# New hand-out order for five engines in an attention and MLP kernel

## The chip, the cores and the metric

The kernel runs on one NeuronCore of a Trainium2 chip. The metric is the device time of one launch in microseconds. Before the change the median of three runs is 753.31 us (754.21, 751.6 and 753.31). A core has five engines that matter here: TensorE (PE, matrix products; the profile shows its weight loads apart, as PEld), VectorE (DVE), ScalarE (ACT), GpSimd (POOL) and SyncE (SP), which in this kernel does nothing but issue transfers. Each engine works through its own instruction stream in the order written and stops where an instruction waits for another engine or for a transfer.

## The reference

A block with conditional layer norm, memory-augmented attention and a squared-ReLU MLP, batch 1, 2048 tokens, width 512, 32 heads of width 16, attention in four segments of 512 tokens, MLP width 1792, all in float32:

```python
mod = (_silu(c) @ w_mod).reshape(...)             # sa, ca, ga, sb, cb, gb
h = _layernorm(x) * (1 + ca) + sa
for s in range(4):                                # segments
    logits = qs @ ks^T * scale + causal mask      # 512 x 512 for each of 32 heads
    a_dot = softmax(logits) @ vs
    a_mem = (phi(qs) @ M) / (phi(qs) @ z + 1e-6)  # memory of the earlier segments
    o = g * a_mem + (1 - g) * a_dot
    M, z = M + phi(ks)^T @ vs, z + sum(phi(ks))
x = x + ga * (o @ wo)
h = _layernorm(x) * (1 + cb) + sb
x = x + gb * (relu(h @ w1 + b1)^2 @ w2 + b2)
```

## The kernel before, in words

**Precision and products.** A float32 factor of the large products is split into a high and a low part, and three products (high·high, high·low, low·high) stand in for one. The projections (`bqk` line 797, `bv` line 867), the output projection (`bwop` line 1287) and the MLP's second product (`bpf` lines 1591 to 1593) do this directly. The MLP's first product (`bh` line 1529) is done by seven products of half-size sums of blocks instead of eight, each of them six matmuls in one PSUM bank.

**Attention.** The work goes by segment and by groups of eight heads, and inside those by quads of four heads. `a_quad` scores a quad once (`ba`, line 905) to find the row maxima: DVE masks and reduces (line 910), the maxima are turned on PE (`bat`, line 970) and brought by SP into the row of the operand tile `ST` that subtracts them (line 978, `ST<-mt`). `b_quad` scores again with the maximum in place (`bpb`, line 1074), ACT takes the exponential (line 1091, `pt`), POOL zeroes what is above the diagonal (line 1078), and PE multiplies with V (`bpv`, line 1133) and turns the result (`bfin`, line 1168). The operands come as follows: `bqk` writes 64 rows at a time in two halves, with an empty ACT node between them (`fence`, line 771) so that the second half starts after the first has finished; ACT and DVE split the result into `sg` (lines 828 and 830), and SP lays it into `ST` with 192 transfers (line 846, `ST<-sg`). `mem` (line 983) reads the memory (`bmr`), turns phi of the keys (`bpkt`, line 1023) and adds to the memory (`bmu`, line 1035).

**MLP.** For each segment and each of seven pairs of 128 columns, `ffn1` gives seven `bh` products; ACT (line 1555) and DVE (lines 1548 and 1552) read each of them out of its bank and add them up, DVE squares (line 1565) and splits (line 1575) the result, and `ffn2` adds it into four output banks, one per 128 tokens, held for the whole segment. The weights of a pair are prepared earlier: POOL and DVE form the sums and SP writes them to memory and fetches them again (line 753, `w1d<-X1L`).

**What sets the order.** The kernel is described as a graph of 3935 nodes, each a few instructions of one engine. `Plan.run` (line 295) walks through it in a time of its own and writes down an order, and `Plan.emit` (line 392) issues the instructions in that order, with nothing else deciding. Which node an engine takes next is not left to priorities: the table `ORDER` (line 57) lists, for each of the five engines, its nodes by number, and the engine takes the next of its list when what the node needs is ready and the buffers it wants are free:

```python
given = self.given.get(e, ())
if turn[e] < len(given):
    n = self.nodes[given[turn[e]]]
    n = n if n in ready[e] and self.can(n) else None
    turn[e] += n is not None
```

Buffers and PSUM banks are handed out first in, first out (`take`, line 280), so another order also gives other buffer numbers to the same work. There are eight banks in all.

Of the kernel before, what the change touches and what calls it, by code (L numbers as in the profile page):

```python
# [69 lines left out]
1498-1499 1208 1240 1500-1501 1236 1144 1248 1503-1504 1243 1331 1505 1220 1506 1325 1481 1338 1482 1346 1483 1560  # L70
1484 1328 1322 1252-1254 1256 1486 1259 1263 1487 1349 1488 1334 1489 1343 1617 1352 1618 1515 1619-1620 1266 1271
1523 1622-1624 1355 1529 1625 1520 1275-1277 1752-1753 1368 1279 1371 1754-1755 1536 1544 2039 2043 1757 1375 1557
1378 1758 1526 1759 1383 1760 1547 2035 2047 1387 1532 1550 1563 1388-1389 1541 1650 1692 1391 1887 1398 1888 1401
1889 1655 1394 1890 1664 1406 1892 1661 1410 1566 1893 1569 1894 1553 1895 1658 1671 1411-1412 1676 1573 1576 1685
1695 1585 1682 1581 1586 1589 1827 1667 1587 1698 1592 1679 1596 1599 1414 1785 1608 1604 1790 1701 1609 1830 1793
1704 1610 1708 2051 1711 1799 2052 1716 2053 1688 2054 1806 1820 1612 1720-1721 1833 1722 1724 1814 2056 1727 2057
1796 1731 2058 1734 1962 1739 2059 1817 1802 1743-1745 1811 2080 1920 1928 2081 1836 2082 1823 2083 1934 1843 1747
2085 1851 2086 1846 2087 1839 2088 1925 2209-2210 1931 2156 1941 2211-2212 1949 1937 1855-1857 1955 1859 2214 1952
2215 2114 2216 1965 2217 2119 1862 2097-2098 1866 2099-2100 1946 1869 2102 1874 2103 1958 2125 2104 2135 2105 2149
2146 496 1878-1880 1971 2128 2333 1974 2334 1978 2140 2335 2122 2336 1981 1882 2338-2339 1986 2143 2340 2131 2341 2259  # L80
2270 1990-1992 1994 2264 2457 2152 2458 1997 2273 2001 2459-2460 2004 2280 2009 2462-2463 2238 2246 2013 2267 2159
2464-2465 2243 2162 2014-2015 2166 2249 498 2169 2017 2174 2178 2182 2185 1968 2179 2252 2276 2180 2189 2192 2404 2197
2599 2615 2201 2362 2255 2202-2203 2373 2602-2604 2367 2605 2205 2607-2608 2283 2609-2610 2290 2631 2293 2618-2619
2376 2620-2621 2286 2370 2623-2624 2298 2625-2626 2634-2635 2383 2397 2636-2637 2379 2647 2302-2304 2486 2494
2639-2640 2306 2641-2642 2500 2663 2313 2650-2652 2321 2653 2666-2667 2316 2668 2491 2669 2655-2656 2391 2657-2658
2309 2671-2673 2497 2674 2407 2727 2679 2325-2327 2730-2733 2410 2388 2414 2735-2738 2682 2394 2683 2422 2684-2685
2743 2687 2400 2688 2507 2689-2690 2521 2746-2749 2417 2329 2751-2752 2430 2753 2433 2754 2426 2515 2503 2437 2695
2800 2796 2804 2792 2427 2449 2428 2759 2440 2698-2699 2445 2700-2701 2518 2531 2703-2705 2512 2706 2534 2711
2450-2451 2762 2538 2524 2763-2765 2453 2546 2767-2768 2541 2769-2770 2714-2716 2554 2557 2717 2775 2550-2551 2561
2564 2719-2721 2528 2569 2722 2552 2573-2575 2778-2781 2577 2783-2786 2934 2933 2935 2839 2936-2937 2859 2842-2845  # L90
2849 2862 2829 2863 2938 2864 2852 2865 2939 2832-2833 2853-2854 2834 2855 2835 2957 2956 2958 2961 2959-2960 2962
3176 3097 2979 3094 2982 3095 2980 3096 2984 3099-3100 2981 3098 3104 3164 2983 2985 3101 3106 3002-3003 3102 3008
3004 3110 3112 3111 3005-3007 3108 3026 3114 3025 3028 3116 3027 3172 3113 3118 3031 3030 3029 3115 3119 3168 3122
3048 3117 3050 3049 3123 3053 3120-3121 3051 3054 3125 3052 3071 3129 3073 3072 3124 3077 3127 3126 3131 3074 3076
3133 3130 3128 3135 3204 3132 3136 3134 3075 3206 3139 3137 3207 3140 3208 3141 3144 3205 3145 3143 3138 3148 3231
3149 3209 3147 3156 3210 3153 3429 3142 3225-3226 3146 3227 3150 3229 3228 3230 3352 3421 3159 3246 3249 3247 3354
3351 3248 3433 3252 3358 3251 3250 3353 3267 3355 3357 3268-3269 3425 3271 3365 3270 3370 3363 3272 3359 3288 3273
3356 3289 3361 3291 3367 3290 3369 3374 3368 3293-3294 3372-3373 3378 3292 3371 3312 3376-3377 3309 3314 3311 3310
3382 3375 3381 3313 3380 3330 3333 3379 3386 3331 3315 3385 3384 3390 3332 3336 3383 3387-3388 3394 3334 3389 3335
3391 3462 3461 3690 3393 3465 3463 3398 3392 3682 3397 3395 3402 3464 3678 3396 3400 3399 3404 3467 3406 3466 3416  # L100
3401 3482 3405 3413 3483-3484 3486 3485 3403 3407 3410 3488 3487 3504 3508 3609-3610 3505 3503 3507 3608 3509 3611
3506 3612 3615 3524 3527 3526 3525 3614 3620 3616 3613 3529 3626 3622 3528 3546 3686 3618 3627 3624 3530 3628 3549
3630 3625 3545 3629 3632 3548 3547 3551 3631 3550 3636 3634 3567 3635 3638 3633 3637 3566 3568-3569 3571 3642 3641
3639 3645 3570 3588 3572 3587 3590 3649 3589 3646 3640 3643 3592 3644 3653 3591 3648 3647 3719 3593 3651 3650 3721
3652 3654 3656 3718 3655 3720 3657 3724 3658-3659 3723 3662 3722 3739 3660 3741 3740 3742 3663 3673 3664 3745 3661
3670 3667 3744 3743 3868 3763 3761 3760 3867 3872 3762 3765-3766 3871 3865 3764 3869 3866 3870 3781 3877 3783 3875
3873 3784 3782 3879 3785-3786 3882 3884 3881 3787 3803 3883 3802 3804 3808 3888 3892 3887 3886 3806 3805 3807 3891
3895 3826 3890 3885 3896 3823 3900 3825 3889 3894 3824 3899 3827-3828 3893 3897 3844 3829 3903 3898 3902 3848 3904
3901 3907 3846 3845 3847 3906 3849-3850 3908 3910 3912 3905 3911 3914 3916 3909 3913 3918 3924 3920 3930 3915 3919
3927 3917 3921  # L110
""",
    "ACT": """
1 4 57 65 96 106 79-80 84 87-88 92 116 108 98 250 118 120 122 100 256 102 258-259 409 110 414 416 310 309 418-419 295
128 112 6 568 301 300 304 303 302 306-307 330-331 326-327 305 131 573 575 578 352 577 278 351 138 357 356 364 363
366-367 436 435 290 360 359 287 286 288 283 289 284 371 285 372 347-348 141 694 838 834 830-831 511 510 835 457 456
380 383 382 379 377 387 386 145 390 699 452-453 701 389 481 395 842 394 704 839 703 595 594 400 636-637 148 843 516
515 522-523 518 849 519 155 526 530-531 763 525 762 473-474 854 615 860 857 489 856 616 863 862 536 539 158 546 545
541-542 538 548 611-612 1018 549 505 721 720 554 553 162 507 559 642 641 648-649 1023 1029 652 651 1032 1031 882
# [1530 lines left out]
```

## Time and profile before

| | before |
|---|---|
| median of three runs | 753.31 us (751.6 to 754.21) |
| span of the profiled execution | 748.9 us |
| instructions in it | 18830 |
| PE busy | 736.3 us (98%) |
| PEld busy | 602.8 us (80%) |
| DVE busy | 585.4 us (78%) |
| ACT busy | 433.4 us (58%) |
| POOL busy | 320.9 us (43%) |

The profile is of one execution, and its own time is its span, 748.9 us. The median of the runs stands 4.4 us above it. Line numbers are those of the kernel before. In the rows of a timeline the first two numbers are the start and the length in microseconds; "x4" is the number of instructions put together in the row, and a bracket at the end is the time that the engine stood idle before it and what it waited for. SPq is SP issuing a transfer. The first 430 us are mostly attention, with weight preparation beside it; from 450 us on it is the MLP.

### The profile page before, as it was taken

The page shows a single profiled execution, that of the slowest core. Times are in us where ns is not written, and L with a number is a line of the kernel's source. Part 1 is how long each engine was busy: PE and PEld are TensorE (multiplying, and loading weights), DVE is VectorE, ACT ScalarE, POOL GpSimd, SP SyncE. Part 2 cuts the span into 40 slices and gives each one's busy share as a digit, 9 for nine tenths or more (in the row PEclk, how much of TensorE's full clock was granted, in tenths as well). Part 3 has the DMA queues.
Part 4 walks back from the last instruction along what each step waited for, and adds up shares of the span by engine and source line. Part 5 has one row for each costly group of instructions (what it writes and reads, how often), then busy time and mean ns, then how long its engine had stood idle before and what let it go on. Part 6 is the DMA issues. An engine that isn't in the chain of part 4 may idle for free.

```text
span 748.9 us, 18830 instructions
## 1 busy us (share of the span) xinstructions
PE 736.3 (98%) x7045; PEld 602.8 (80%) x7045; DVE 585.4 (78%) x1597; ACT 433.4 (58%) x971; POOL 320.9 (43%) x400
## 2 busy tenths in 40 slices
PE   8999999999999999999999999999999999999997
PEld 7876778666877678675888789998998898989986
DVE  5587897989899888799999868878766775576544
ACT  2669888899979987788768835562312311221110
POOL 5667858589968787374324433241020002000000
PEclk9999999999999999999999999999999999999999
DMA  9777763446645354547721366753644354538721
GB/s 310 230 236 238 243 198 90 133 136 191 172 136 136 93 140 139 126 131 221 220 79 59 123 222 248 271 208 107 222 163 181 119 208 182 184 131 280 269 94 56
DMA packets 61060, 129.70 MB, mean 173 GB/s; under 512 B 8613, under 2 KB 23977, under 8 KB 59178
## 3 DMA queue, kind: packets, MB, share of 16 engines
q1 hardware_dynamic: 60818, 128.37, 53.8%
q8 instruction: 56, 0.92, 0.5%
q14 instruction: 34, 0.28, 0.1%
q10 hardware_dynamic: 152, 0.13, 0.1%
HBM read 81.29 MB, written 20.19 MB: 136 GB/s over the span
## 4 chain that ended last, share of the span: by engine, by line
PE 77%; DMA 6%; POOL 4%; ACT 4%; issue 3%; SPq 3%; DVE 2%; POOLq 0%; ACTq 0%
PE bh L1529 19%; PE bpv L1133 7%; PE bpf L1592 7%; PE bpf L1591 7%; PE bpf L1593 7%; PE bqk L797 6%; PE bpb L1074 5%; PE bwop L1287 5%; PE ba L905 4%; PE bv L867 4%; DMA w1d<-X1L 2%; SPq L846 2%; ACT pt L1091 1%; PE bwot L1261 1%; POOL WQK L711 1%
## 5 line engine op out<-in xcount | busy, mean ns | idle before, releaser
L910 DVE CUSTOM_DVE_ANT_0 ba<-ba,msk 128x384 f32<-128x384 f32 (+2 forms) x384 | 192.4, 532 | 25.1 <-PE ba L905 13.7
L1091 ACT ACTIVATE pt<-bpb 128x512 f32<-128x512 f32 x320 | 172.5, 617 | 14.9 <-PE bpb L1074 13.2
L1078 POOL TENSOR_SCALAR_AFFINE_SELECT pt<-pt 128x512 f32<-128x512 f32 x128 | 79.1, 636 | 72.3 <-ACT pt L1091 62.1
L797 PE MATMUL bqk<-HT,WQK 64*128 64x512 f32 x720 | 103.9, 396 | 0.0
L1133 PE MATMUL bpv<-pt,VT 128*32 128x128 f32 (+3 forms) x1024 | 81.1, 437 | 1.1 <-ACT pt L1091 0.4
L1074 PE MATMUL bpb<-ST 64*128 64x256 f32 (+2 forms) x512 | 79.1, 344 | 1.4 <-ACT pt L1091 0.4
L797 PEld LDWEIGHTS bqk<-HT,WQK 64*128 64x128 f32 x720 | 71.4, 185 | 8.8 <-issue 0.9
L905 PE MATMUL ba<-ST 63*128 63x256 f32 (+2 forms) x512 | 76.4, 340 | 2.0 <-DMA ST<-sg 1.3
L1074 PEld LDWEIGHTS bpb<-ST 64*128 64x128 f32 x512 | 51.5, 185 | 20.8 <-ACT pt L1091 4.3
L1573 ACT CAST ST<-xx 128x512 fp32r<-128x512 f32 x43 | 26.5, 620 | 69.3 <-DVE xx L1565 55.0
L905 PEld LDWEIGHTS ba<-ST 63*128 63x128 f32 x512 | 51.0, 185 | 18.5 <-issue 4.9
L1529 PEld LDWEIGHTS bh<-ST 128*128 128x128 f32 x420 | 56.5, 189 | 3.6
L1529 PE MATMUL bh<-ST 128*128 128x256 f32 x420 | 59.2, 282 | 0.0
L1529 PEld LDWEIGHTS bh<-ST,w 128*128 128x128 f32 x420 | 55.7, 190 | 3.1
L1529 PE MATMUL bh<-ST,w 128*128 128x256 f32 x420 | 57.7, 282 | 0.0
L867 PE MATMUL bv<-WVO,HT 64*128 64x512 f32 x384 | 56.9, 397 | 0.0
L1360 POOL TENSOR_TENSOR tt<-h2raw 128x512 f32<-128x512 f32 x8 | 11.0, 1388 | 102.8 <-ACT h2raw L1325 77.6
L1133 PEld LDWEIGHTS bpv<-pt,VT 128*32 128x32 f32 x1024 | 28.1, 109 | 33.4 <-issue 22.8
L910 DVE DVE_READ_ACCUMULATOR2_ANT mx<- 128x1 f32 x384 | 54.2, 141 | 0.0
L1591 PE MATMUL bpf<-w,ST 128*128 128x512 f32 x132 | 52.2, 396 | 0.0
L1592 PE MATMUL bpf<-w,ST 128*128 128x512 f32 x132 | 52.0, 394 | 0.0
L1593 PE MATMUL bpf<-w,ST 128*128 128x512 f32 x132 | 51.7, 391 | 0.0
(204 smaller groups left out, 1600.7 us busy)
## 6 DMA issues: line engine op xcount, KB each, us to landing
ST<-w1d SPq DMA_DIRECT2D x14, 1792.0 KB
w<-w1d SPq DMA_DIRECT2D x14, 1792.0 KB
ST<-sg SPq DMA_DIRECT2D x192, 128.0 KB
w1d<-X1L SPq DMA_DIRECT2D x21, 512.0 KB
xt<-in_A_x SPq DMA_DIRECT2D x16, 256.0 KB
wm<-in_w_mod SPq DMA_DIRECT2D x16, 256.0 KB
xw<-in_A_x SPq DMA_DIRECT2D x16, 256.0 KB
X1L<-in_B_w SPq DMA_DIRECT2D x7, 512.0 KB
```

Of the source, the lines that this page charges most:

```text
L797: nc.tensor.matmul(bank(banks[w]), W3(w, k, x, cols.start, cols.stop)[r], HT[r, y, k], start=first and i == 0, stop=last and i == 2)
L867: nc.tensor.matmul(bank(banks[t]), HT[r, x, k, (t2 + t) * P:(t2 + t + 1) * P], WVO[r, k, y], start=first and i == 0, stop=last and i == 2)
L905: nc.tensor.matmul(dst[:, c0:c0 + n], ST[b:b + 63, 0, sl, qt * P:(qt + 1) * P], ST[b:b + 63, 1, sl, :n], start=True, stop=True)
L910: nc.vector.tensor_tensor_reduce(i, i, msk[:, 512 - n:], scale=1.0, scalar=-3e38, op0=ALU.add, op1=ALU.max, accum_out=o)
L1074: nc.tensor.matmul(dst, ST[b:b + 64, 1, sl, kb * P:(kb + 1) * P], ST[b:b + 64, 0, sl, q0:512], start=True, stop=True)
L1078: nc.gpsimd.affine_select(out=ap, in_=ap, pattern=[[0, ap.shape[1]], [1, P]], compare_op=ALU.is_ge, fill=0.0, base=0, channel_multiplier=-1)
L1091: ns = [op("ACT", 0.49, lambda j=j: nc.scalar.activation(buf("PPP"[n], pt)[:, i + j], bank(keys[j]), AF.Exp, scale=0.25), pr[slot] + 0.01 ...
L1133: nc.tensor.matmul(bank(o)[32 * hq:32 * hq + 32, q0:q0 + src.shape[1]], v[:, a:a + 32], src, start=start, stop=stop, tile_position=(0, 32 ...
L1529: nc.tensor.matmul(pb(i), A[:, x, kk], B[:, y, kk], start=kk == j == 0, stop=kk == 1 and j == 2)
L1591: nc.tensor.matmul(q, rh, wh, start=(i == 0), stop=False)
L1592: nc.tensor.matmul(q, rh, wl, start=False, stop=False)
L1593: nc.tensor.matmul(q, rl, wh, start=False, stop=(i == NF - 1))
```

## The change

Only the table `ORDER` is replaced. The five new lists hold the same nodes, each on the same engine; the graph, the instructions of each node, the buffers and every constant stay. The lists are the result of another search over the same plan, one in which the durations of the nodes were drawn anew again and again instead of being fixed.

The diff is 337 lines long, nearly all of it numbers; its head:

```diff
 ORDER = {
     "PE": """
-8-30 3 31-33 56 34-37 58 64 82 78 38 66 39-40 90 86 41-47 246-249 252-255 405-408 291 410-413 292-293 308 322 294
...
+8-24 3 25-33 56 34-37 58 64 38-39 82 78 66 90 40-43 86 44-47 252 246-249 253-255 405-408 410-413 291-293 308 294 322
...
```

Compared as lists, PE has 1325 nodes, of which 696 stand at another position, most of them by one to three places and at most by 25; of its 1324 pairs of neighbours 568 are kept. On ACT 642 of 955 nodes have moved, on DVE 643 of 907 (by up to 66 places), on POOL 261 of 342, on SP 346 of 403 (by up to 46). Between the products that use full precision in different ways PE changes over 140 times in the old list and 142 times in the new one. In the built programs PE has 327 separate wait instructions before and 313 after. Three places follow.

**First place: SP, about 290 to 305 us.** These are transfers into the operand tile (`ST<-sg`, line 846), the maxima's rows (`ST<-mt`, line 978), a write of prepared weights (`w1d<-X1L`, line 753), the modulation weights (`wm`, line 564) and the attention output on its way through memory (`o_dram<-on`, line 1195). Before:

```order
L978 DMA ST<-mt 1x8x128 x2
L564 DMA wm<-in_w_mod 128x512
L846 DMA ST<-sg 32x2x512 x3
L564 DMA wm<-in_w_mod 128x512 x2
L846 DMA ST<-sg 32x2x512 x2
L564 DMA wm<-in_w_mod 128x512
L753 DMA w1d_136<-X1L 256x1x512
L846 DMA ST<-sg 32x2x512 x3
L1195 DMA o_dram<-on 128x4x128
L846 DMA ST<-sg 32x2x512 x3
L978 DMA ST<-mt 1x8x128 x2
```

And now:

```order
L978 DMA ST<-mt 1x8x128 x2
L564 DMA wm<-in_w_mod 128x512
L846 DMA ST<-sg 32x2x512 x4
L1195 DMA o_dram<-on 128x4x128
L846 DMA ST<-sg 32x2x512 x3
L978 DMA ST<-mt 1x8x128 x2
L846 DMA ST<-sg 32x2x512 x3
L753 DMA w1d_136<-X1L 256x1x512
```

Between the two pairs of `ST<-mt` the weight write is gone (it stands behind them), three of the four `wm` loads are elsewhere, and seven fills are listed instead of eleven. The fill of line 846 that stands first in the last row of three of the old list, the 15th transfer after the first pair, is in the new list the third of the row of three, the ninth transfer after it; the PE node that uses it, a `ba` pair, stands two nodes earlier in PE's list.

**Second place: PE, about 45 to 56 us.** `ba`, `bpb` and `bpkt` are the attention products named above, `bv` the projection of V. Before:

```order
L867 MATMUL bv<-WVO,HT 128x512 x12
L905 MATMUL ba_686<-ST 128x512
L905 MATMUL ba_687<-ST 128x512
L867 MATMUL bv<-WVO,HT 128x512 x6
L1023 MATMUL bpkt<-ident,phi_377 128x64 x8
L867 MATMUL bv<-WVO,HT 128x512 x6
L905 MATMUL ba_736<-ST 128x256
L905 MATMUL ba_737<-ST 128x256
L905 MATMUL ba_736<-ST 128x384
L905 MATMUL ba_737<-ST 128x384
L1074 MATMUL bpb<-ST 128x512 x2
```

And now:

```order
L867 MATMUL bv<-WVO,HT 128x512 x12
L905 MATMUL ba_690<-ST 128x512
L905 MATMUL ba_691<-ST 128x512
L867 MATMUL bv<-WVO,HT 128x512 x12
L1023 MATMUL bpkt<-ident,phi_448 128x64 x8
L1074 MATMUL bpb<-ST 128x512 x2
L867 MATMUL bv<-WVO,HT 128x512 x6
L1074 MATMUL bpb<-ST 128x256 x2
L1074 MATMUL bpb<-ST 128x384 x2
L1074 MATMUL bpb<-ST 128x256 x2
L1074 MATMUL bpb<-ST 128x384 x2
L867 MATMUL bv<-WVO,HT 128x512 x6
```

Two groups of `bv` stand ahead of `bpkt` instead of one, and the four `ba` that followed it stand behind the end of the `bpb` shown.

**Third place: PE in the MLP's last segment.** `bh` is the first product, six matmuls to a bank, and `bpf` the second. The longest row of `bh` with the four output banks in use was, before, five:

```order
L1593 MATMUL bpf<-w_8752,rr 128x512
L1529 MATMUL bh<-ST,w_10254 128x256 x6
L1529 MATMUL bh<-H2o_6297,ST 128x256 x6
L1529 MATMUL bh<-ST,w_10254 128x256 x6
L1529 MATMUL bh<-H2o_6296,ST 128x256 x6
L1529 MATMUL bh<-ST 128x256 x6
L1591 MATMUL bpf<-w_8752,ST 128x512
```

And now there is one of eight (the two rows of x12 are two products each):

```order
L1593 MATMUL bpf<-w_8885,ST 128x512
L1529 MATMUL bh<-ST 128x256 x6
L1529 MATMUL bh<-H2o_6295,ST 128x256 x6
L1529 MATMUL bh<-ST 128x256 x6
L1529 MATMUL bh<-H2o_6294,w_10644 128x256 x6
L1529 MATMUL bh<-ST 128x256 x12
L1529 MATMUL bh<-ST,w_10644 128x256 x12
L1591 MATMUL bpf<-w_8885,ST 128x512
```

These are not the same eight products: the segment's 49 are divided into rows in another way.

More of the change, by code (lines that the diff above doesn't have):

```diff
@@ new lines @@
+2671-2674 2497 2727 2679 2325-2327 2407 2730 2388 2731-2733 2410 2414 2735-2736 2394 2737-2738 2682-2685 2422 2743
+2687 2400 2688 2507 2689-2690 2521 2746-2749 2417 2329 2751-2752 2430 2753 2433 2754 2426 2515 2503 2437 2695 2800
+2804 2796 2792 2427-2428 2449 2759 2445 2698 2440 2699-2701 2518 2531 2703-2706 2534 2512 2711 2450-2451 2762-2763
+2524 2538 2764-2765 2546 2453 2767-2768 2541 2769-2770 2714-2716 2554 2717 2557 2775 2550-2551 2719 2561 2720-2721
+2564 2722 2528 2569 2552 2573-2575 2778-2781 2577 2783-2786 2935 2933-2934 2839 2937 2859 2936 2842-2843 2849
@@ new lines @@
+3652 3720 3718 3656 3655 3650 3659 3721 3657 3722-3724 3654 3658 3663 3662 3660 3741 3664 3670 3739 3673 3742 3740
+3744 3760 3743 3745 3762 3764 3661 3868 3667 3866 3761 3870 3865 3763 3765 3872 3869 3766 3867 3879 3875 3781 3871
+3877 3884 3782 3883 3785 3783 3787 3784 3786 3882 3806 3803 3802 3886 3873 3887-3888 3881 3804-3805 3808 3807
+3890-3891 3829 3885 3824 3827 3823 3889 3893 3826 3825 3897 3895 3892 3896 3850 3844 3828 3900 3894 3899 3903 3898
+3845-3846 3902 3847 3907 3901 3904 3849 3908 3848 3912 3916 3906 3911 3905 3915 3920 3909 3930 3910 3919 3927 3914
@@ L111 @@
+3918 3913 3924 3917 3921
 """,
     "ACT": """
[L113 to L116, printed above, removed]
@@ new lines @@
+2310-2311 2680 2728 2328 2409 2408 2734 2411 2415-2416 2412 2686 2424 2744 2401-2402 2423 2509 2508 2750 2419 2418
+2431-2432 2435 2434 2504-2505 2438 2696 2801 2797 2805 2793 2439 2429 2760 2447 2446 2442 2702 2441 2533 2532 2819
+2535 2712 2536 2815 2811 2452 2525-2526 2539 2766 2547 2540 2548 2543 2813 2542 2556 2821 2817 2776 2718 2558-2559
+2555 2563 2562 2565-2566 2570-2571 2576 2553 2823 2782 2940 2840 2860 2850 2880 2830 2948-2949 2871 2950 2875
+2952-2953 2963 2954 3177 2971 2986 2884 2972-2973 2975 2916 2994 2976 2995 2977 3165 3009 2889 2893 2998-3000 2898
@@ L190 @@
[L190 to L191 removed]
+2 68-69 71 70 74-76 59 77 67 83 91 81 85 89 93 251 117 820 257 821 415 417 823 324 323 320-321 317 312 315 822 318 314
+339 338 342 341 576 574 335-336 827-828 333 825 344-345 450 826 449 438 444 443 447 446 441 440 513 459 464-465 7 700
+470 702 471 608-609 483 354 461-462 468 467 602-603 402-403 597 599-600 855 861 605 639 606 491 629-630 618 1423 1426
@@ new lines @@
+2225 2120 2118 2121 1948 1947 2127 2126 2148 2147 2150-2151 2139 2130 2129 2141-2142 2124 2123 1884 1883 2144-2145
+2343 2272 2349 2271 2266 2265 2274-2275 2263 2281-2282 2248 2247 2268-2269 2245 2244 2242 2251 2250 2582 2018 2586
+1969 2019 2590 2594 2584 2253 2473 2254 2588 2406 2405 2467 2601 2596 2592 2617 2374-2375 2368-2369 2207 2206
+2611-2612 2366 2633 2378 2377 2372 2627 2371 2628 2398-2399 2387 2649 2495-2496 2643 2502 2644 2665 2501 2490
+2492-2493 2393 2392 2659 2645 2675-2676 2498-2499 2729 2660-2661 2681 2389-2390 2629 2208 2613 2396 2739 2395 2740
@@ new lines @@
+3298 3427 3284 3300-3302 3317 3303 3306 3318-3319 3677 3874 3320 3322 3308 3321 3323 3305 3338-3339 3445 3340 3324
+3441 3443 3689 3342 3447 3344 3327 3326 3449 3348 3453 3341 3343 3345 3329 3469 3681 3451 3470 3472 3617 3347 3471
+3473 3366 3350 3474-3475 3692 3490-3491 3680 3479 3476 3493 3495 3414 3492 3411 3478 3494 3496-3497 3481 3500 3408
+3511-3512 3502 3417 3513 3499 3515 3514 3684 3517 3521 3532 3516 3533 3518 3876 3520 3535 3523 3537 3534 3536
+3538-3539 3688 3553-3554 3556 3541 3555 3558 3557 3542 3559 3563 3565 3574 3544 3575 3577 3576 3578 3560 3580 3878
@@ new lines @@
+3562 3579 3704 3581 3595 3700 3583 3596-3598 3708 3600 3584 3599 3586 3706 3601 3702 3605 3698 3726-3727 3607 3710
+3729 3621 3728 3602 3604 3730 3732 3736 3738 3731 3733 3665 3747-3750 3735 3752 3880 3674 3751 3671 3753-3754 3757
+3768-3769 3756 3771 3770 3772-3773 3668 3759 3775 3774 3789 3778 3780 3790 3792 3791 3794 3793 3795 3777 3810 3796
+3811-3812 3799 3813 3801 3814-3815 3798 3817 3816 3820 3831-3832 3822 3834 3833 3835 3837 3819 3841 3836 3838 3852
+3843 3853 3855 3840 3854 3857 3859 3856 3858 3862 3861 3864 3931 3928 3933 3925 3922
@@ new lines @@
+2351 2356-2357 2360 2359 2354 2353 2155 2581 2589 2585 2593 2358 2350 2361 2355 2598 2614 245 2630 2279 2480 2258 2476
+2483 2478 2646 2484 2662 2474 2482 2475 2477 2485 2481 2021 2678 2726 2382 2694 2742 2710 2479 2403 2758 2868 2506
+2774 2527 2858 2827 2878 2869 2838 2826 2873 2848 2877 2828 2886 2914 2882 2896 2895 2931 2891 2887 2904-2905 2900
+2913 2909 2923 2918 2922 2927 3197-3200 3161 3155 3201-3203 3454-3458 3152 3459-3460 3711-3714 3158 3715 3669 3409
+3415 3666 3716 3418 3717 3675 3932 3412 3672 3929 3926 3923
```

261 lines of the change are left out of this document (112 added, 149 removed), and 14 rows, old and new, of the table ORDER.

## The prediction

> **What bounds the kernel now.** I read the stages first, to see which engine leaves no room and where.
>
> ```profile
> core 0: us, PE busy (x) PEld busy (x) DVE busy (x) ACT busy (x) POOL busy (x), PEclk, DMA share, GB/s
> 0.00:60.00 60.00, 56.32 (x441) 47.76 (x441) 39.99 (x101) 33.66 (x81) 38.85 (x58) 1.00 0.83 258
> 60.00:180.00 120.00, 117.83 (x1499) 83.50 (x1498) 104.55 (x358) 105.91 (x247) 90.33 (x108) 1.00 0.59 173
> 180.00:300.00 120.00, 118.73 (x1448) 89.67 (x1448) 105.82 (x354) 102.71 (x244) 94.83 (x126) 1.00 0.51 139
> 300.00:430.00 130.00, 128.40 (x1668) 98.91 (x1661) 119.49 (x361) 101.44 (x226) 55.92 (x78) 1.00 0.47 136
> 430.00:560.00 130.00, 130.00 (x867) 117.58 (x864) 101.46 (x199) 52.67 (x105) 33.68 (x27) 1.00 0.59 209
> 560.00:748.90 188.90, 185.06 (x1141) 165.34 (x1139) 114.08 (x228) 36.95 (x73) 7.27 (x5) 1.00 0.47 169
> ```
>
> PE sets the time in every stage. Its idle time is 3.7, 2.2, 1.3, 1.6, 0.0 and 3.8 us, 12.6 in all, and the last 3.8 are the drain after the last product. An order cannot shorten the products, so what it can win by is this idle time and what PE loses inside its busy time. The MLP from 430 us on has no idle to give; it can only lose. In attention DVE is at 87%, 88% and 92% of the three stages from 60 us, so a wait removed there can easily come back behind DVE.
>
> Next, what PE and its weight loads waited for:
>
> ```profile
> PE bwarm L544 <- POOL ident masks.py:199: 1.9, 1, 1.9
> PE ba L905 <- DMA ST<-sg: 1.3, 2, 1.1
> ...
> PEld bpv L1133 <- issue: 22.8, 103, 0.5
> PEld bpv L1133 <- POOL pt L1078: 7.1, 22, 0.8
> ```
>
> The three numbers are the total, the count and the longest. The start-up wait of 1.9 us is before the order matters. The 1.1 us for a transfer is the longest that an order can move; the rows left out are shorter, 0.7 us at most. The 22.8 us over 103 loads are 0.22 us each, and nothing released them: it is what PE pays when it changes between the full-precision products and `bpv`. The 7.1 us are waits for POOL's selects that the matmul before mostly covers.
>
> **The change part by part.** The instructions are the same, so no term comes from work added or removed. I cost the places at which PE stands still, then those at which the new list may make it stand.
>
> *The first place, 305 us.* PE and SP there:
>
> ```profile
> 304.70 0.64 PE L905 MATMUL ba<-ST 63*128 63x256 f32 x4 [1.08 <-DMA ST<-sg]
> ...
> 289.23 1.30 SPq L978 DMA_DIRECT2D ST<-mt  x2
> ...
> 296.32 1.14 SPq L753 DMA_DIRECT2D w1d<-X1L  x1
> ...
> 300.40 0.59 SPq L1195 DMA_DIRECT2D o_dram<-on  x1
> 301.04 1.91 SPq L846 DMA_DIRECT2D ST<-sg  x3
> ...
> L1477 SPq DMA_DIRECT2D ST<-w1d x14: 523/524/581, 416.4 to 701.7; - x14
> ```
>
> (The last line is SP's summary of the transfers that read the prepared weights: their count, lengths in ns, and the first and last start.) The queue issues one transfer after the other here, so the late fill is late by its position. It is the first of the three issued from 301.04 and PE starts on it at 304.70. In the new list eight transfers stand between the `ST<-mt` pair and it instead of 14: six fewer, at (301.04 − 289.23 − 1.30)/14 = 0.75 us each, some 4.5 us earlier. PE also wants it earlier, by the two nodes that it moved up; a six of `bqk` or `bv` takes 0.70 us (worked out below), so by about 1 us. What is left is over three times the wait of 1.08 us: I take −1.1. If the data itself is later than the queue, the bounds are −1.1 and +0.5, that is, PE asking 1 us earlier and winning half of it only. The weight write moves behind it; the first reader of such weights comes at 416.4 us, so a write late by 10 us is still covered; with that cover gone it would cost its own 1.14 us.
>
> [...]
>
> *The second place, 46 to 56 us:*
>
> ```profile
> 46.65 0.50 PE L905 MATMUL ba<-ST 63*128 63x512 f32 x1 [0.34 <-DVE mx L910]
> 48.60 0.40 PE L1023 MATMUL bpkt<-ident,phi 64*128 64x64 f32 x6 [0.75 <-DVE sg L830]
> 50.85 0.92 PE L867 MATMUL bv<-WVO,HT 64*128 64x512 f32 x6
> 51.90 0.86 PE L867 MATMUL bv<-WVO,HT 64*128 64x512 f32 x6
> 53.34 0.56 PE L1074 MATMUL bpb<-ST 64*128 64x256 f32 x3 [0.42 <-ACT pt L1091]
> 55.16 0.39 PE L905 MATMUL ba<-ST 63*128 63x256 f32 x2 [0.23 <-DMA ST<-sg]
> ```
>
> 1.74 us of idle stand here. One more group of `bv` now stands ahead of `bpkt`; it fills about 0.70 us (the six from 51.90 gave way to `bpb` at 52.60), nearly all of the 0.75. The `ba` that waited 0.23 us for its fill stands later by several groups, so that goes as well. The other two I leave: the `bpb` now come sooner after the scores that feed them and their 0.42 us can as well double. I take −0.70 − 0.23 = −0.9; bounds −1.7 (all) and +0.4 (the `bpb` wait doubled and the work pulled forward missing later, which undoes the 0.7).
>
> *Two smaller waits of the same kind:*
>
> ```profile
> 66.68 0.90 PE L1074 MATMUL bpb<-ST 64*128 64x512 f32 x4 [0.32 <-DMA ST<-mt]
> 141.75 1.07 PE L1133 MATMUL bpv<-pt,VT 128*32 128x512 f32 x8 [0.23 <-ACT lnf L631]
> ```
>
> At the first a group of `bmu` now stands ahead of the `bpb` that waits, at the second a pair of `bpb` (four of the size in the first row are 0.90 us) ahead of the `bpv`. I take all of both but 0.05, −0.5; bounds −0.55 and 0 (the cover shifted, not won).
>
> *The rest of the attention.* More than half of PE's neighbours are new (568 of 1324 pairs kept), so the small waits are dealt anew. Selects stand earlier in the lists between 180 and 360 us by about 0.7 us on average and later by about as much between 60 and 180 us; I get these shifts from the lists' positions with the durations of the rows. The wait rows hold 7.1 us over 22 for selects, 0.32 us each; the later half gains and the earlier half loses, but the earlier one is also where PE idles more (2.2 us against 1.3), so I give −0.3 in all, bounds −3.5 (half of the 7.1) and +3.5 (the same on the other side). Fourteen wait instructions fewer on PE are worth
>
> ```profile
> L1529 PEldq EVENT_SEMAPHORE  x5: 51/51/51, 605.3 to 635.9; - x5
> ```
>
> 0.051 us each, −0.7 if every one of them lay bare. Most lie under a matmul; I take −0.3, bounds −0.7 and 0.
>
> *What it costs.* Two more changes of mode at 0.22 us each are +0.4. In two of the projection's fences less work lies between the halves:
>
> ```profile
> 28.17 1.12 PE L867 MATMUL bv<-WVO,HT 64*128 64x512 f32 x6
> 29.14 2.22 PE L797 MATMUL bqk<-HT,WQK 64*128 64x512 f32 x18
> ```
>
> These six `bv` filled one such gap; in the new list the halves follow each other there. PE waits for its own result and the empty ACT node, which I price by the nearest rows, the waits of 0.3 to 0.75 us above: +0.5, less the 0.2 by which the `bv` fit better elsewhere, +0.3, bounds 0 and +0.75. The other fence keeps most of its filling.
>
> *The MLP.* A bank is held until DVE or ACT has read it, and with four output banks in use four are left. Before, five in a row went through without a wait:
>
> ```profile
> 647.60 0.86 PE L1529 MATMUL bh<-ST,w 128*128 128x256 f32 x6
> ...
> 650.40 0.87 PE L1529 MATMUL bh<-ST 128*128 128x256 f32 x6
> ...
> L1552 DVE SCALAR_TENSOR_TENSOR u<-bh,b1c,u 128x256 f32<-128x256 f32 x56 | 26.9, 480 | 9.9 <-PE bh L1529 8.9
> L1565 DVE SCALAR_TENSOR_TENSOR xx<-xx 128x512 f32<-128x512 f32 x42 | 28.8, 695 | 0.3
> L1575 DVE TENSOR_TENSOR ST<-xx,ST 128x512 fp32r<-128x512 f32 x43 | 32.0, 745 | 7.8 <-ACT ST L1573 7.7
> ```
>
> The first and the fifth start (650.40 − 647.60)/4 = 0.70 us apart each. DVE reads one in 0.48 at most, so DVE keeps pace unless a square and a split (0.695 and 0.745) stand in its list between two reads. In the row of eight the last four need four returns; one square and split in between put DVE 1.4 us behind, of which the slack of 0.22 us per read takes back 0.9 to 1.0 over the four free banks. That leaves +0.4 for the row of eight, and nothing for the rows of five and six, which is the length that ran clean or one more. I take +0.4, bounds 0 and +1.4.
>
> *Start and end.* The two halves of the drain stay: the last product, its addition on DVE and the last store are the same nodes. One load of the first tokens is issued eighth instead of fifth on SP, three issues of about 0.65 us, under a stage where PE idles for the identity anyway; 0 here, bounds 0 and +0.5.
>
> **Sum:** −1.1 − 0.9 − 0.5 − 0.3 − 0.3 + 0.4 + 0.3 + 0.4 = −2.0 us. Against the profiled execution that is 748.9 → 746.9; the runs shown have a median 4.4 above their profile, so I apply it to the median: 753.3 − 2.0 = 751.3, which is what I predict. A measurement of this kernel can tell about 0.3%, 2.3 us, from no change: faster begins at 751.0 and slower at 755.6. The forecast lies on the edge of that.
>
> **Rivals.**
>
> *The waits only change places (R1).* DVE and ACT are busy for 86 to 88% of 60 to 300 us, and −2.5 of the sum are waits closed while others are dealt anew. For it: those rows. Against it: the first place is a queue position and not an engine's load. Then only the costs of mode, fence and bank stay beside that place: −1.1 + 1.1 = 0, 753.3.
>
> *The small waits shrink together (R2).* If half of the select waits (3.5 us) and all of the second place (0.8 more than taken) go, the gain is 2.0 + 3.2 + 0.8 = 6 us: 747.3. For it: PE idles at named waits in attention at many places, and over half of the pairs are new. Against it: the later selects in the first third.
>
> *The MLP begins to wait (R3, slower).* It has 0.0 us of idle in 430 to 560 us, and its banks pass through DVE at 78% of that stage. If DVE's new list puts squares and splits ahead of bank reads, each such place costs up to the 1.4 us worked out above; with a loss of that size at four of the 28 column pairs beyond the one taken, 5.6 us come on top: 753.3 − 2.0 + 5.2 = 756.5 (the 0.4 taken out). It decides from the point at which PE's idle between 430 and 745 us passes 4.7 us (2.4 gained elsewhere and 2.3 to be told from no change). For it: the row of eight. Against it: on average DVE has 28 us left in that stage.
>
> *Selects late in the first third (R4, slower).* If the 0.7 us by which they stand later between 60 and 180 us is met at ten of the 22 waiting places, it costs 7 us, of which the later places give back 2, in place of the −0.3 taken: 753.3 − 2.0 + 0.3 + 5 = 756.6. The profile has POOL idle there for a quarter of the stage, against it.
>
> [...]
>
> **How the numbers follow.** The forecast (749.3 to 752.8) has 0.38, R1 0.16, R2 0.22, R3 0.14, R4 0.08, R5 0.02. Faster by over 0.3% is R2 and 0.22 of the forecast's 0.38, since the sum's bounds reach well below that edge (every lower end together makes −7.1): 0.44. Within 0.3% is the rest of the forecast, most of R1, and R5: 0.16 + 0.13 + 0.02 = 0.31. Slower is R3, R4 and 0.03 of R1: 0.25. The range takes in R2, R3 and R4 with some room, since the bounds of the selects alone are ±3.5: 745.0 to 758.0. The likeliest case's own range is 749.3 to 752.8.
>
> **What would show it.** The bracket of 1.08 us at `ba` near 305 us gone, with the fill issued some 4 us ahead; `bpkt` near 48 us without its 0.75; the first stage with PE idle at 2.8 us instead of 3.7; 130.0 us of PE busy in 430 to 560 us still, and `bh` with a wait of at most 0.5 us in the row of eight; about 105 loads with the price of a mode change. I am wrong if PE's idle in the MLP grows past 4 us (R3), if `bpv` waits for POOL much above 7.1 us (R4), or if idle in attention stays at its 8.8 us although these places are clean (R1).

## The result and the profile after

| | before | after |
|---|---|---|
| median of the runs | 752.13 us (65 runs, 749.02 to 754.99) | 746.22 us (10 runs, 745.4 to 747.54) |
| ratio after to before, first four runs of each | | 0.9925 (0.990 to 0.995) |
| ratio later, 6 runs against 18 | | 0.9923 (0.9905 to 0.9942) |
| span of the profiled execution | 748.9 us | 743.8 us |
| PE busy | 736.3 us (98%) | 733.7 us (99%) |

The change makes the kernel faster by 5.9 us, 0.8%. The forecast was 751.3 us, 2.0 us faster, with a range of 745.0 to 758.0. The measured time lies in that range, near its lower end, and outside the likeliest case's own range of 749.3 to 752.8. Two later runs, one of the old kernel (1002.86 us at a granted clock of 0.66) and one of an experiment (879.28 us at 0.75), are left out of all medians and ratios. The same stages of the kernel after, in the columns of before:

```profile
0.00:60.00 60.00, 56.35 (x457) 48.92 (x459) 42.44 (x110) 35.70 (x85) 42.36 (x61) 1.00 0.88 265
60.00:180.00 120.00, 118.07 (x1522) 83.50 (x1522) 104.67 (x352) 107.00 (x246) 90.73 (x109) 1.00 0.59 171
180.00:300.00 120.00, 119.56 (x1456) 89.42 (x1450) 107.76 (x361) 102.19 (x244) 89.46 (x122) 1.00 0.51 140
300.00:430.00 130.00, 129.78 (x1688) 101.94 (x1685) 120.20 (x362) 100.84 (x227) 59.27 (x78) 1.00 0.50 145
430.00:560.00 130.00, 130.00 (x829) 117.09 (x828) 95.99 (x190) 51.68 (x102) 33.74 (x27) 1.00 0.59 212
```

PE's idle time between 60 and 430 us is 2.6 us; it was 5.0. The first 60 us have 3.65 us of it, as much as before (3.68), and the prediction had named 2.8 as a sign: new waits stand there in place of the old ones. From 430 to 560 us, in the MLP, there is none, before and after. The waits of PE and of the weight loads after, as total, count and longest:

```profile
PE bwarm L544 <- POOL ident masks.py:199: 1.9, 1, 1.9
PE bpb L1074 <- DMA ST<-mt: 1.4, 1, 1.4
...
PEld bpv L1133 <- issue: 24.4, 110, 0.4
PEld bpv L1133 <- POOL pt L1078: 4.3, 15, 0.8
```

The wait of 1.1 us for an operand fill is gone, and there is a new one of 1.4 us for the maxima of a quad. The weight loads' waits for selects fell from 7.1 us to 4.3.

Where the time went can be read off the same piece of work in both traces. PE rows of the kernel before, start and length in us:

```profile
10.95 1.06 PE L572 MATMUL bmod<-wmod,cs 128*32 128x512 f32 x8
44.49 1.60 PE L867 MATMUL bv<-WVO,HT 64*128 64x512 f32 x12
60.15 1.53 PE L627 MATMUL blnq<-ident,xt 128*128 128x128 f32 x12
71.78 1.06 PE L572 MATMUL bmod<-wm,cs 128*32 128x512 f32 x8
100.38 1.08 PE L998 MATMUL bmr<-MB,phi 64*128 64x68 f32 x16
298.93 2.36 PE L1133 MATMUL bpv<-pt,VT 128*32 128x512 f32 x32
305.85 0.40 PE L1023 MATMUL bpkt<-ident,phi 64*128 64x64 f32 x7
450.24 1.52 PE L1529 MATMUL bh<-H2o,w 128*128 128x256 f32 x12
744.67 0.39 PE L1593 MATMUL bpf<-w,ST 128*128 128x512 f32 x1
```

And the same after (the row of `bh` is the first with both factors written that way; some earlier `bh` lie before it in both traces):

```profile
10.07 1.06 PE L572 MATMUL bmod<-wmod,cs 128*32 128x512 f32 x8
44.10 1.60 PE L867 MATMUL bv<-WVO,HT 64*128 64x512 f32 x12
58.10 1.53 PE L627 MATMUL blnq<-ident,xt 128*128 128x128 f32 x12
68.76 1.41 PE L572 MATMUL bmod<-wm,cs 128*32 128x512 f32 x8
98.17 1.03 PE L998 MATMUL bmr<-MB,phi 64*128 64x68 f32 x16
295.13 2.36 PE L1133 MATMUL bpv<-pt,VT 128*32 128x512 f32 x32
300.63 0.40 PE L1023 MATMUL bpkt<-ident,phi 64*128 64x64 f32 x8
444.96 1.53 PE L1529 MATMUL bh<-H2o,w 128*128 128x256 f32 x12
739.51 0.40 PE L1593 MATMUL bpf<-w,rr 128*128 128x512 f32 x1
```

The lead of the new kernel at these marks is 0.88, 0.39, 2.05, 3.02, 2.21, 3.80, 5.22, 5.28 and 5.16 us. So it is won in four places: 1.66 us between 44 and 60 us (the second place of the prediction), 0.97 between 60 and 72, 1.59 in many small steps between 100 and 299, 1.42 at 305 us (the first place). It loses 0.49 between 11 and 44 us, 0.81 between 72 and 100 us and nothing worth naming in 290 us of MLP. The drain after the last product is the same: 743.8 − 739.51 and 748.9 − 744.67 are 4.3 and 4.2 us. The first 0.88 us belong to the warm-up and are taken up below.

Idle time is only part of it. Between the first mark and the last the new kernel is 4.28 us shorter. Summed over these stretches, PE's idle time falls from 6.81 to 4.33 us, that is by 2.48, and its busy time by 1.80, for the same products. Between 44 and 60 us the idle time falls by 0.37 us only and the busy time by 1.29, so time is lost there between products that the rows show as busy. Four `ba` that start at 49.86 us in the old kernel are followed by the next row after 0.65 us, without a bracket, and four of the same size at 57.67 us after 0.30. The weight loads point the same way: their listed waits in this stretch fall from 4.0 to 2.3 us. What releases these products was not taken apart.

One pair of traces is little for the first 60 us. In the other traces that have the old lists there, unaltered, the stretch from 44 to 60 us takes 15.93, 16.27 and 17.25 us (15.66 above), and with the new lists 13.81, 14.22, 14.56 and 16.33 us (14.00 above). The three longest, 16.27, 16.33 and 17.25, hold a lowered clock: 0.68 from 50 to 53 us, 0.59 from 52 to 56 us and 0.83 from 50 to 60 us. So the gain there is more than chance, but its size is known to about a microsecond only. The stretch from 11 to 44 us takes 33.54 to 33.57 us in four traces with the old lists and 33.94 in a fifth, and 33.94 to 34.97 with the new ones, so the loss there holds too.

The profiled executions are 5.1 us apart and the medians 5.9. The device time of a run is its span and some 1.7 us (745.48 and 743.8 for the profiled one after), so the span of 748.9 belongs to a run of about 750.6 us, 1.5 us under the median of before, while the profiled run after is 0.7 us under its own: the trace of before was a lucky one, and a comparison of these two traces shows a little less than the comparison of many runs. The 753.31 us of three runs, from which the forecast started, was in turn 1.2 us above the median of 65.

### The profile page after: what moved, and what is told of

It reads as the page before. It is cut to its first block, busy times and chain, and to the rows that moved or that the text cites. A ratio compares the mean times of both kernels' runs of the same rounds, so it can differ in the third digit from the quotient of the medians.

```text
span 743.8 us, 18809 instructions
## 1 busy us (share of the span) xinstructions
PE 733.7 (99%) x7045; PEld 601.8 (81%) x7045; DVE 584.1 (79%) x1597; ACT 434.3 (58%) x971; POOL 322.3 (43%) x400
## 4 chain that ended last, share of the span: by engine, by line
PE 87%; DVE 5%; ACT 3%; DMA 2%; issue 1%; SPq 1%; POOL 0%; ACTq 0%; DVEq 0%; POOLq 0%
PE bh L1529 19%; PE bqk L797 9%; PE bpv L1133 8%; PE bpf L1592 7%; PE bpf L1591 7%; PE bpf L1593 7%; PE bv L867 6%; PE ba L905 5%; PE bpb L1074 5%; PE bwop L1287 3%; DVE ba L910 2%; PE bwarm L544 2%; PE bmr L998 1%; ACT pt L1091 1%; PE blnq L618 1%
## 5 line engine op out<-in xcount | busy, mean ns | idle before, releaser
L1074 PE MATMUL bpb<-ST 64*128 64x256 f32 (+2 forms) x512 | 80.8, 345 | 2.3 <-DMA ST<-mt 1.4
L1133 PE MATMUL bpv<-pt,VT 128*32 128x512 f32 (+3 forms) x1024 | 81.4, 438 | 0.3 <-ACT lnf L631 0.2
L1555 ACT COPY p<-bh 128x256 f32<-128x256 f32 x28 | 10.4, 371 | 80.0 <-PE bh L1529 66.8
L1133 PEld LDWEIGHTS bpv<-pt,VT 128*32 128x32 f32 x1024 | 27.6, 109 | 32.3 <-issue 24.4
L1591 PE MATMUL bpf<-w,ST 128*128 128x512 f32 x120 | 47.6, 397 | 0.0
L1592 PE MATMUL bpf<-w,ST 128*128 128x512 f32 x120 | 47.3, 394 | 0.0
```

The source lines that it names most:

```text
L1074: nc.tensor.matmul(dst, ST[b:b + 64, 1, sl, kb * P:(kb + 1) * P], ST[b:b + 64, 0, sl, q0:512], start=True, stop=True)
L1133: nc.tensor.matmul(bank(o)[32 * hq:32 * hq + 32, q0:q0 + src.shape[1]], v[:, a:a + 32], src, start=start, stop=stop, tile_position=(0, 32 ...
L1591: nc.tensor.matmul(q, rh, wh, start=(i == 0), stop=False)
L1592: nc.tensor.matmul(q, rh, wl, start=False, stop=False)
```

## The experiments

**One transfer on SP.** The old kernel, with the fill that PE waited for at 305 us issued six places earlier:

```diff
 "SP":
-... 495 2072 2069 494 232 2078-2079 2075 1616 2068 2073 2077 1940 ...
+... 495 2072 2069 2068 494 232 2078-2079 2075 1616 2073 2077 1940 ...
```

> The old kernel with one transfer moved: the operand fill that PE waited for at 305 us is issued six places earlier on SP, nothing else moves. Theory (it was late by its place in the queue): the wait of 1.08 us goes and 1.1 to 1.4 us with it, span 747.6 us. [...] Rival (the next wait takes its place): 748.9 us.

Measured: 750.84 against 752.27 us, ratio 0.9974 (0.9959 to 0.9989), that is 1.4 us between the medians; profiled span 748.3 us. PE around the place:

```profile
303.73 0.85 PE L797 MATMUL bqk<-HT,WQK 64*128 64x512 f32 x6
304.42 0.40 PE L905 MATMUL ba<-ST 63*128 63x256 f32 x4
```

The bracket of 1.08 us is gone and none stands in its place. The queue's position was the cause. Between the marks `bpv` and `bpkt` this kernel takes 305.35 − 299.88 = 5.47 us, against 6.92 in the old kernel and 5.50 in the new one: this one node is worth there what all five new lists are worth. The span is only 0.6 us shorter, since this trace is 0.95 us later at the first of these marks, and as much already at 290 us, ahead of the moved transfer.

**One group of products on PE.** The old kernel, with the `bv` group ahead of the turn of phi:

```diff
 "PE":
-... 276 350 277 343 355 279 ...
+... 276-277 350 343 355 279 ...
```

> The old kernel with one PE node moved: the group of six projection products that followed the turn of phi at 48.6 us stands ahead of it, as in the new list. Theory by the step of the prediction (the group fills the wait): 0.7 us gained, span 748.2 us. Rival (the same group is then missing behind the turn, where the scores wait for their maxima): nothing, 748.9 us, with the bracket moved to the next row of scores.

Measured: 751.24 against 751.96 us, ratio 0.9994 (0.9975 to 1.0014): no difference that the runs show, though the 0.7 us of the theory lie inside that interval too. Of its ten runs 8 had a mean granted clock under 0.999, of the old kernel's 22 beside them 7. Its rows:

```profile
47.17 0.47 PE L905 MATMUL ba<-ST 63*128 63x512 f32 x1 [1.03 <-DVE mx L910]
50.17 0.46 PE L1023 MATMUL bpkt<-ident,phi 64*128 64x64 f32 x7 [0.29 <-DVE sg L830]
51.43 0.79 PE L905 MATMUL ba<-ST 63*128 63x256 f32 x4 [0.80 <-DVE mx L910]
52.59 0.67 PE L1074 MATMUL bpb<-ST 64*128 64x512 f32 x2 [0.37 <-DMA ST<-mt]
```

The wait at `bpkt` shrank from 0.75 to 0.29 us, and the scores behind it wait 0.80 us where nothing stood before, as the rival had it: the group that fills one gap opens the next. The wait of 1.03 us stands ahead of the moved group and is not its work. Without it the stretch from 44 to 60 us takes 15.65 us, as in the old kernel (15.66). In the new kernel the place is another one altogether:

```profile
47.13 0.43 PE L1023 MATMUL bpkt<-ident,phi 64*128 64x64 f32 x8
48.97 0.64 PE L1074 MATMUL bpb<-ST 64*128 64x512 f32 x2 [1.41 <-DMA ST<-mt]
49.28 1.04 PE L867 MATMUL bv<-WVO,HT 64*128 64x512 f32 x6
...
51.27 0.63 PE L905 MATMUL ba<-ST 63*128 63x256 f32 x4
```

One long wait for a quad's maxima stands in place of the short ones at `ba`, `bpkt`, `bpb` and `ba`, and after it no bracket stands up to the mark at 58.10 us. This one node does not bring the gain of 1.66 us; which other nodes, on which engines, are needed was not taken apart.

**New lists early, old lists late, and the reverse.** First with the join at about 77 us on all five engines:

```diff
 all five lists:
+the nodes that the new order hands out before PE's node 466, in the new order
 then the rest in the old order
```

> All five lists are the new ones up to the same PE product at about 77 us, and the old ones from there. Theory (the gain is a sum of separate PE stalls, each keeping its own share): PE stands 2.6 us ahead of the old kernel at the join, and keeps it, so a span of 748.9 - 2.6 = 746.3 us; 0.8 of that comes from the warm-up products reaching the full clock earlier, and if that is the phase of the clock and not the order, it may be missing: 747.1. Rival (what is won early is lost again at the next busy producer): the lead shrinks between 77 and 430 us and the span is 748.5 to 749.2.

> The other half: old lists up to about 77 us, new ones from there. Theory of separate stalls: 5.2 - 2.6 = 2.6 us gained, of which 1.4 at about 305 us: span 746.3 us. Rival (waits only move on, and the early lead is needed for the later ones): 748.0 or more; the other rival (the later lists carry everything): 744.5 or less.

Measured: 754.18 us for the first (ratio 1.0029, 1.0012 to 1.0046: slower than the old kernel) and 750.77 for the second (0.9976, 0.9956 to 0.9997), against 752.27. Neither theory had this. The first kernel's longest wait, and its stages of 4 us around it:

```profile
PE ba L905 <- ACT pt L1091: 3.0, 1, 3.0
...
82.00:86.00 4.00, 3.79 (x52) 3.06 (x48) 3.80 (x13) 0.80 (x3) 3.19 (x5) 1.00 0.86 263
86.00:90.00 4.00, 0.98 (x4) 0.57 (x2) 0.04 (x1) 2.03 (x5) 1.27 (x1) 0.75 0.71 224
90.00:94.00 4.00, 4.00 (x23) 2.21 (x26) 2.68 (x8) 3.17 (x10) 2.50 (x4) 0.50 0.37 135
94.00:98.00 4.00, 4.00 (x106) 2.04 (x100) 2.12 (x8) 3.06 (x7) 1.96 (x2) 0.90 0.89 283
```

A wait of 3.0 us stands behind the join, and from it on the granted clock (third number from the end) is 0.75, 0.50 and 0.90 of full. The second kernel waits 2.4 us at the same kind of product, about 90 us, and its clock is 0.83 from 90 to 100 us. Neither the old nor the new kernel has such a wait there: between 80 and 98 us their longest are 0.56 and 0.22 us, and the clock is 1.00. So the two orders do not fit together at this seam, and these two kernels say nothing on whether the gains add up, and something else on the clock, below. So the join was moved to about 105 us, ahead of PE's node 640:

> The join of new and old lists again, now at about 105 us, where the two orders stand closer together on every engine. Theory (separate stalls): PE is 2.2 us ahead at the join and keeps it, 752.1 - 2.2 = 749.9 us, or some 749.4 if the first 60 us also lose the clock less often. Rival (an early lead is lost at the next busy producer): 751.5 to 752.5. If the join itself stalls PE as the one at 77 us did, a wait of over 1.5 us stands right behind it in the rows, and the run says nothing on either.

> The other half: old lists until about 105 us, new ones from there. Theory: 5.2 - 2.2 = 2.9 us gained, 749.2 us, 1.4 of it at 305 us, and the clock as often reduced in the first 60 us as in the old kernel. Rival (the whole gain belongs to the start): 751.5 or more.

Measured, against 752.21 us: 749.11 us (ratio 0.9953, 0.9933 to 0.9973) and 748.74 us (0.9961, 0.9946 to 0.9975). The two gains are 3.1 and 3.5 us, 6.6 together, where the whole change wins 6.0 beside the same old runs; the difference lies inside the intervals. So each side of 105 us has its part of the gain, and the two parts add up within the scatter. The idea that an early lead is lost again at the next busy producer falls. The profiled execution of the first is no typical one (span 748.3 us, with a wait of 2.5 us for `ST<-mt`), so its share between the stages is not read from it.

**The MLP's lists.** New lists up to about 385 us, old ones from there:

> New lists up to about 385 us, old lists from there, the MLP's among them. Theory (the MLP's new order is worth nothing, the whole gain lies in attention): the lead of 5.6 us at the join is kept, span 743.3 us, and the row of eight products without a wait is gone with no effect. Rival (the MLP's lists share in the gain): 745 us or more. If the long rows had cost something: 743.0 or less.

Measured: 745.98 against 752.27 us (ratio 0.9911, 0.9883 to 0.9938), span 744.0 us, with the new kernel at 746.22 and 743.8. The old and the new order of the MLP are worth the same as far as four runs can tell. The span of 743.3 was missed by 0.7. In this trace, as in the new kernel's, the last product starts 294.6 to 294.7 us after the mark at 445 us, so the MLP is not the reason. In the new kernel the row of eight products runs like this:

```profile
671.18 0.88 PE L1529 MATMUL bh<-ST 128*128 128x256 f32 x6
...
674.00 1.58 PE L1529 MATMUL bh<-ST 128*128 128x256 f32 x12
675.42 1.60 PE L1529 MATMUL bh<-ST,w 128*128 128x256 f32 x12
```

From the first to the seventh product (675.42 − 671.18)/6 = 0.71 us apart, and no bracket: four banks were enough for eight in a row.

**Repairing the new kernel.** Its longest wait, 1.41 us for `ST<-mt`, stands behind a load of modulation weights and a fill on SP. First the maxima ahead of these two:

```diff
 "SP":
-... 125 430 476 432 328 427 133 ...
+... 125 430 328 476 432 427 133 ...
```

> The new kernel with one transfer moved: at 44 us the maxima of the first quad are issued ahead of a load of modulation weights and one operand fill instead of behind them, some 1.8 us earlier. Theory (one stall, one gain): the wait of 1.41 us that PE has there goes, span 743.8 - 1.4 = 742.4 us. Rival (the fill that is now later, or the next maxima, stops PE instead): 743.5 us or more.

then also a `bv` group put back between the halves of the projection at 28 us:

```diff
 "PE":
-... 405-408 410-413 291-293 308 ...
+... 405-408 291 410-413 292-293 308 ...
```

> As the kernel before it, and the group of projection products stands between the two halves of the projection at 28 us again, as in the old order. Theory: another 0.35 us, the bracket of 0.34 us at the second half goes: 742.1 us. Rival (the group is missing at 30 to 40 us): no change against the one before.

and both with the old lists from 385 us:

> The two repairs of the new kernel at 28 and 44 us, and the old lists from about 385 us. Theory (separate stalls add up): 743.8 - 1.4 - 0.35 - 0.5 = 741.5 us, the fastest of all. Rival (they do not add): 742.5 us or more.

Measured: 745.36, 745.32 and 746.47 us against 751.96 (ratios 0.9928, 0.9923 and 0.9936, each give or take 0.002 to 0.003). None differs from the new kernel's 0.9923. The first kernel's rows, in the slowest of its four runs:

```profile
47.70 0.69 PE L1074 MATMUL bpb<-ST 64*128 64x512 f32 x2
...
52.96 0.38 PE L905 MATMUL ba<-ST 63*128 63x256 f32 x2 [0.89 <-ACT pt L1091]
54.01 0.80 PE L905 MATMUL ba<-ST 63*128 63x256 f32 x6 [0.66 <-DMA ST<-sg]
54.60 1.49 PE L797 MATMUL bqk<-HT,WQK 64*128 64x512 f32 x6
```

The wait of 1.41 us is gone, and 0.89 + 0.66 = 1.55 us stand 5 us later. That the repair moved the wait is not shown: two other traces with the new lists unrepaired up to there also wait for the fill at 54 us, 0.47 and 0.64 us, and in one of them the wait at `bpb` is 0.72 us instead of 1.41. In the second kernel, the `bv` group that should fill the fence has no weights yet:

```profile
28.46 0.73 PE L867 MATMUL bv<-WVO,HT 64*128 64x512 f32 x4 [0.84 <-POOL WVO L711]
```

0.84 us lost to save the 0.34 that the new kernel pays there. From 11 to 44 us this kernel takes 34.44 us, inside the 33.94 to 34.97 of the new lists, so filling the fence won nothing. Last, the repair on SP alone with the old lists from 385 us:

> The new kernel with the first quad's maxima issued earlier on SP at 44 us and the old lists from about 385 us, the fence left as in the new list. Theory: the first repair kept about half of its 1.4 us, since scores at 53 us then wait for 0.9; the join at 385 us is worth 0 to 0.5: 745.2 us, ahead of the new kernel by about 1. Rival: no difference from the new kernel, 746.2 us or more.

Measured: 747.04 against 752.21 us (0.9927, 0.9906 to 0.9949). Its profiled execution has the shortest span of all, 742.1 us, and its runs go from 743.81 to 748.14 us: one run is no verdict here. The theory's 745.2 us did not come. No version was found that beats the new kernel.

**The new kernel again, for the clock.**

> The new kernel itself beside the same old runs, for the clock: in 19 of 47 runs the old kernel had a mean granted clock under 0.999, and those were 1.3 us longer in the median. Theory (shorter waits in the first 60 us keep the clock up): at most 2 of 10 runs under 0.999, median 746.3 us, and the gain among full-clock runs alone is 5 to 6 us. Rival (the clock is luck and has no part): 4 of 10 under 0.999.

Measured: 746.22 against 752.21 us (0.9923, 0.9905 to 0.9942); 2 of its 6 runs had a mean granted clock under 0.999, and with the first four runs it is 3 of 10. The old kernel had 26 of 65. That is too few runs to tell the two apart, so the theory that the new order keeps the clock up is not borne out. Among runs at 0.999 or more the medians are 751.69 (39 runs) and 745.95 us (7): the gain is 5.7 us with the clock left out.

## Why the prediction was right, and where its sum was off

The direction and the place where the gain lies (attention only) were right, and of its kind (PE waits closed, one by one) about half: 2.5 of the 4.3 us between the first mark and the last are idle time, the other 1.8 lie inside PE's busy time, for which the sum had 0.2. The size was not right: 2.0 us forecast, 5.9 measured. The time fell into the stated range because that range was made wide enough for R2 and the selects; the likeliest case's own range missed it. Of the named signs the bracket at 305 us, `bpkt` and the MLP came true, the first stage's 2.8 us of idle did not (3.65). By the terms of the sum:

- **First place, −1.1.** Measured −1.42 in the traces and 1.4 us when done alone. Right, a little small: what the other 0.3 us are was not taken apart. The late place in the one queue was the cause: moving it alone won 1.4 us (0.8 to 3.1).
- **Second place, −0.9.** Measured −1.66 between 44 and 60 us, give or take about a microsecond. The step that failed is "One more group of `bv` … fills about 0.70 us": done alone it moved the wait and won nothing in the trace. The brackets of 1.74 us did go, but as a whole place set anew, and a new wait of 1.41 us came with it, so the idle time won is 0.37 us. The other 1.29 us lie inside PE's busy time, where no bracket shows them and the prediction had put nothing for this place.
- **Two smaller waits, −0.5.** The first lies in the stretch from 60 to 72 us, which won 0.97 us, as two more waits before it (0.18 and 0.17 us at `ba` and `bpkt`) went too; 0.52 us of this is idle time, 0.45 busy time. The second, of 0.23 us at `bpv`, did not go: it reads 0.17 us after, although the `bpb` do stand ahead of it. The term was half of what was there, and in part right by luck.
- **The rest of the attention, −0.6 with the wait instructions.** +0.81 us between 72 and 100 us and −1.59 between 100 and 299, −0.8 in sum: near, as a small difference of two larger shares of opposite sign, which is the shape that was argued (later selects first, earlier ones then). Whether the selects make them was not tested; the loads' waits for selects fell by 2.8 us (7.1 to 4.3), more than the stretch won.
- **Mode changes, +0.4.** The rows went from 22.8 us over 103 to 24.4 over 110, so +1.6 us of load waits, part of them under the matmul before. The reading behind the term does not hold: counted in the timeline of the weight loads, only 22 of the 103 rows (4.8 us) follow another product, and the other 81 stand between loads of `bpv` itself, so most of them are no price of a change. The 22 are no longer than the others, 0.22 us each in both groups, so no run shows such a price for them either. What they are is open; the marks do not show this term apart, and it was not tested.
- **Fence, +0.3.** The lead falls from 0.88 to 0.39 us between the marks at 10.95 and 44.49 us, +0.49, and the new bracket at the second half of the projection reads 0.34 us. Right, if a little small.
- **MLP, +0.4.** The lead goes from 5.28 to 5.16 us, that is +0.1, and the experiment shows no difference. The row of eight ran without a wait.
- **Start, 0.** The 0.88 us at the first mark are not counted as the order's; see below.

The traces differ by 5.2 us from the start of PE to its end, 3.2 more than the sum. Of these, 0.8 lie in the second place, 0.5 in the small waits, 0.3 in the first place, 0.2 in the rest of the attention, 0.4 in the mode changes that do not show, 0.3 in the MLP and 0.9 in the warm-up, less 0.2 for the fence: no one large miss by place, but seven small ones of one sign. By kind there is one: −0.2 us were put for what PE loses inside its busy time, the small waits dealt anew, and −1.8 were measured, while the idle time, −1.8 in the sum, came to −2.5. The rest up to 5.9 is the luck of the two traces, 1.5 us before and 0.7 after.

Of the rivals, R2 (the small waits shrink together, 747.3) was nearest. Its two causes were there in part: the waits for selects fell by 2.8 of 7.1 us, though how much of this PE gained is not shown, and the second place won nearly its whole 1.7, though mostly not from the brackets. R1 falls by the time itself and by the joins at 105 us, where each side keeps its gain. R3 falls by the row of eight and the exchanged MLP lists. R4 did not show: waits for selects fell. R5, with its chance of 0.02, stands for a wait of PE that is followed by a lower clock. It did not happen in the new kernel's trace, whose longest wait behind the start, 1.41 us, left the clock at 1.00; in the experiments waits of 3.0 and 2.5 us were followed by a clock of 0.50 and 0.59. From which length on it happens is shown by no run.

## What to carry to other kernels

Where one engine is 98% busy, an order can only win what that engine loses. List its brackets, but do not take them for the whole: here as much again, nearly, lay inside its busy time, and the waits of its weight loads and the distance between the same two products in both traces showed it. For a wait on a transfer compare the issue queue's rows with the time the data was ready; one transfer moved by six places was worth a quarter of this whole change. A group of work moved into a gap can open another gap where it came from, so price both ends, and price a place that several lists set anew as a whole, between nothing and all of its idle time, rather than node by node. Orders that were found together cannot be cut and joined freely: at 77 us one join cost more than its half had won, at 105 and 385 us the joins cost nothing that shows.

## What the runs showed of the hardware

**Waits of 3.0 and 2.5 us on PE were followed by a lower clock, and shorter ones sometimes.** A wait of 3.02 us on PE was followed by 0.50 of the clock from 90 to 94 us (above). All ten runs of that kernel had a mean granted clock under 0.999, of the other kernel joined at 77 us nine of ten, of the old kernel 26 of 65. The kernel with the new lists up to 105 us waited 2.49 us, and its clock was 0.59 from 52 to 56 us. In the first repaired kernel two waits of 0.89 and 0.66 us came before this, in its stages:

```profile
52.00:55.00 3.00, 1.45 (x12) 1.15 (x12) 0.91 (x5) 2.59 (x7) 2.46 (x2) 0.90 0.79 194
55.00:58.00 3.00, 3.00 (x20) 2.48 (x18) 2.93 (x10) 2.27 (x10) 2.74 (x4) 0.53 0.85 261
58.00:62.00 4.00, 4.00 (x38) 3.17 (x38) 2.34 (x9) 3.78 (x9) 2.58 (x4) 1.00 0.90 272
```

In it six `bqk` take 1.49 us (54.60, in the rows above), and 0.86 at 57.94 us in the same trace, where the clock comes back to 1.00. The new kernel's own wait of 1.41 us left the clock at 1.00, and so did waits of 1.35 and 0.64 us, 5 us apart, in its other trace, and one of 1.88 us for `ST<-mt` at 50.52 us in the kernel with the new lists up to 77 us. So it isn't the length of the waits alone that decides. What else does was not taken apart.

**The warm-up ends at another time in every trace.** The first `bmod` after the warm-up products starts at 10.95 us in the trace before and 10.07 in the one after, but over all 14 traces it goes from 10.06 to 11.10 us with the old start and from 9.59 to 10.96 with the new one, and the two ranges overlap nearly whole. From 2 to 4 us there are 10 of the warm-up's matmuls in both traces; 18 or 19 matmuls in two microseconds stand first from 8 to 10 us in the trace before (19) and from 6 to 8 us in the one after (18), with the same instructions up to there. The column of the granted clock reads 1.00 all this time, so that it is the clock, as the expectation of the first join at 77 us has it, is shown by no run. The 0.88 us in the marks are within the scatter of this kind and are not counted as gain.

**The first 60 us scatter.** Among 65 runs of the old kernel the time goes from 749.02 to 754.99 us, and among its runs at 0.999 or more over the same range. The waits of 45 to 56 us differ from trace to trace for the same lists there (the `ba` that starts at 45.89 us in the old kernel waits for nothing, and the same one at 47.17 us in the kernel with a single, later PE node moved waits 1.03 us for `mx`), at a time when the transfer engines are at a share of 0.63 to 0.97 in the trace before. What starts the scatter was not traced.
